# The second factor of a blocked Fourier transform: four separate 32x32 products instead of stacked cosine and sine rows

## The chip, the cores and the metric

The kernel runs on one core of a Trainium2 chip. A core has a matrix engine (PE; its weight loads are listed as PEld), a vector engine (DVE), an activation engine (ACT), a general engine (POOL) and a queue engine (SP); each works through its own instructions in order, and they meet through semaphores. PE writes to PSUM only, and PSUM has eight banks, each holding 512 floats in every one of 128 partitions. The metric is the time of one execution on the device in microseconds (us).

## The reference

The input x has 8 batches of 3008 rows and 256 channels. Each batch is filtered along its rows in the frequency domain, and the result goes through two dense layers with an ELU between them, all in float32.

```python
X = np.fft.rfft(x, axis=1)
Y = X * (filt_r + 1j * filt_i)[None, :, :]
y = np.fft.irfft(Y, n=x.shape[1], axis=1)
h = y.reshape(8 * 3008, 256) @ w_in                       # to 2048
g = np.where(h > 0.0, h, np.exp(np.minimum(h, 0.0)) - 1.0)
return g @ w_out                                          # to 256
```

## The kernel before

**The transform.** 3008 is 64 times 47, so the transform is two factors with a trip through DRAM between them. For one batch: `x_unit` and `a_unit` do the first factor forward (length 64, six pieces c, two to an `a_unit`), and `z_write` puts the result z into DRAM. `z_read` brings back four rows of it for one step g of 0 to 7, `f_read` the filter for that step, `b_unit` does the second factor forward (length 47, folded to 24 cosine and 24 sine rows) and multiplies by the filter. `bi_unit` does the second factor back for two steps together, `y_write` and `y_read` go through DRAM again, and `n_unit` does the first factor back for a sixth of the batch (m of 0 to 5). `n_sums` prepares it for the dense layers.

**The dense layers.** They are done by Strassen-Winograd 2x2 blocks with seven products: `up_steps` gives seven steps s1, s2, s6, s5, s7, s3, s4 of the first layer for a quarter q of the 2048 columns, `down_steps` seven steps of the second layer. A step is two matmul instructions in the code and four in the trace. One pass of seven ups and seven downs is called a quad here: quad i does the ups of item i (b, m, q) and the downs of item i - 1. The steps share PSUM banks: s1, s6, s5 and s3 add up in one bank (phs), s7 and s4 in one (phd), s2 has one (pha). ACT copies phs out after s1, s6 and s5; DVE adds what was copied to pha and phd (L502); ACT takes exponentials in two instructions (L511, L512); DVE takes the maximum (L516); after the steps comes a tail of four DVE sums (L552 to L556). s4 adds into phd only when the DVE add of s7 has read it. DVE adds the second layer's result up in three instructions in the quad after q = 3 and four more in `c_unit`, both at L592, and `o_unit` transposes it (L614, two instructions) and sends it out in 16 DMAs (L624).

**The order.** The order of all instructions is written out by hand. A batch has a period of 24 quads; `at(quad, place, ...)` puts a piece of transform work into a quad, at place 0 (after seven or eight of its 14 steps) or place 1 (at its end). The transform of batch b runs in the 24 quads of batch b - 1's dense layers; below, quads are counted 0 to 23 within that period. The steps go

```python
for k in "DUUDUDDU" if i in opens else "UUDUDDU":    # place 0 follows
for k in "DUUDUD" if i in opens else "DUUDUDD":      # place 1 follows
```

with U an up and D a down. A quad in `opens` begins with a down, which needs none of the four PSUM banks (`banks`, tiles m0 to m3) that ups, `a_unit`, `n_unit`, `b_unit` and `bi_unit` take in turn from the front of one list and return to its end; the other four banks hold the second layer's sums. In a period `a_unit` stands at the end of quads 2, 4 and 7, `b_unit` at the end of quads 9, 10, 12, 13, 15, 16, 18 and 19, `bi_unit` at the end of 11, 14, 17 and 20, and `n_unit` in quads 23, 1, 5, 8, 12 and 16.

**The step that changes.** In `b_unit` a step's input lies in 48 rows twice: cosine rows above sine rows, for the real part (`LO`) and the imaginary part (`HI`). Sixteen matmuls (L376) of 48 rows, 32 columns of weights and 256 moving columns leave both parts in two PSUM banks (psr, psi). DVE multiplies both by both filter parts (`products`, L328 to L331), and POOL does the sums (L385 to L390), with three copies more in step 0 (L393, L395). `z_read` issues four DMAs a step on SP, `f_read` four on POOL.

Of the kernel before, what the change touches and what calls it, by code (L numbers as in the profile page):

```python
# [41 lines left out]
def _make_tables():  # L42
# [53 lines left out]

    fb, bb = np.zeros((P, 2, 2, 32)), np.zeros((P, 2, 4, 32))
    for r in (LO, HI):  # L100
        fb[r, :, 0, :24] = gb[r, :, 0:24]
        fb[r, 0, 1, 1:24] = gb[r, 0, 24:47]
        fb[r, 1, 1, :24] = gb[r, 1, 24:48]
    for o in range(0, P, 32):
        for p, (t, c) in enumerate(((gr, 0), (gr, 24), (gi, 0), (gi, 24))):
            bb[o:o + 24, 0, p, :24] = t[0:24, 0, c:c + 24]

    bb[0:24, 1, 0, :24], bb[0:24, 1, 1, :24] = gr[0:24, 1, 0:24], gr[24:48, 1, 24:48]
    bb[0:24, 1, 2, :24], bb[0:24, 1, 3, :24] = gi[24:48, 1, 0:24], gi[0:24, 1, 24:48]
    pairs = np.concatenate([fb.reshape(P, P), bb.reshape(P, 2 * P)], 1)  # L110
    lie = np.concatenate([2 * np.arange(24), 2 * np.arange(24) + 1])
    gb[:, :, lie] = gb[:, :, :48].copy()
    for t in (gr, gi):
# [15 lines left out]
def kernel(  # L129
# [22 lines left out]
    sdp = pool("sdp", 2)  # L152
    tnp = pool("tnp", 2)
    t1p = pool("t1p", 3)
    t2p = pool("t2p", 2)
    sp = pool("sp", 1)
    qp = pool("qp", 1)
    t3p = pool("t3p", 1)
# [5 lines left out]
    psO = pool("psO", 1, space=PSUM)  # L164
    psM = pool("psM", 1, space=PSUM)

    pairs = glob.tile([P, 3 * P], FP32, name="pairs")
    fb = pairs[:, 0:P].rearrange("p (v c k) -> p v c k", v=2, c=2)
    bb = pairs[:, P:3 * P].rearrange("p (v a i) -> p v a i", v=2, a=4)

    w_in, w_out = ([glob.tile([P, 7, 2, P], FP32, name="%s%d" % (n, i)) for i in range(4)] for n in ("wi", "wo"))

    fbufs = [glob.tile([P, 2, 2, D], FP32, name="f%d" % i) for i in range(FBUFS)]
    edges = glob.tile([P, 2], FP32, name="edges")
    fd = fdp.tile([NG, 2, 48, 2, 2, D], FP32, name="fd")
    fp = fdp.tile([NG, 4, 24, 2, 2, D], FP32, name="fp")

    xs, tas, tns, t1s, t2s, ss, t3s, t4s, zs, yds, ys, g_of, po_of, cs_, sds = ({} for _ in range(15))

    def raw(src, row, ap, col=0):  # L180
        return bass.AP(tensor=src.tensor, offset=src.offset + row * D + col, ap=ap)
# [98 lines left out]

    def t_first(g):

        pool, tag = (t4p, "t4") if g % 4 > 1 else (t2p, "t2")
        t = t2s[0, g] = pool.tile([P, 4, D], FP32, tag=tag, name="t2")
        for j in range(2):
            i = j + 2 * (g % 2 if g < 4 else 0)
            ps = psO.tile([P, 2, 256], FP32, tag="po%d" % i, name="po%d" % i)
            for u in range(2):
                k = 4 * g + 2 * j + u
                for dh in range(2):  # L290
                    nc.tensor.transpose(ps[0:ROWS, u, ts(dh, P)], zt[k // 16][dh][:, ts(k % 16, ROWS)], eye)
            nc.scalar.activation(out=t[0:ROWS, 2 * j:2 * j + 2, :], in_=ps[0:ROWS], func=AXT.Copy)
# [10 lines left out]
            nc.sync.dma_start(z[r], t[HALVES[r]])  # L303

    def z_read(b, g):
        t = t2s[b, g] = t2p.tile([P, 4, D], FP32, tag="t2", name="t2")
        for p, r in enumerate((0, 24, 64, 88)):
            k = p * K2 + 4 * g
            nc.sync.dma_start(t[r:r + 24].rearrange("i u d -> i (u d)"), zs[b][:, k:k + 4, :].rearrange("i u d -> i (u d)"))

    def f_read_first(g, t):
        for a, r in enumerate((LO, HI)):
            nc.gpsimd.dma_start(t[r].rearrange("p c u d -> p (c u d)"), fd[g, a].rearrange("q c u d -> q (c u d)"))

    def f_read(b, g):
        t = fbufs[(b * NG + g) % FBUFS]
        for a in range(4):
            nc.gpsimd.dma_start(t[32 * a:32 * a + 24].rearrange("p c u d -> p (c u d)"),
                                fp[g, a].rearrange("q c u d -> q (c u d)"))
# [47 lines left out]


    def b_unit(b, g):
        t = t2s.pop((b, g))  # L370
        f = fbufs[(b * NG + g) % FBUFS]
        (i0, re), (i1, im) = (bank(n) for n in ("psr", "psi"))
        for c in range(2):
            for a in range(4):
                for ps, k in ((re, LO), (im, HI)):
                    nc.tensor.matmul(ps[32 * a:32 * a + 32, c, :], fb[k, 1 if g == a == 0 else 0, c, :], t[k, a, :],  # L376
                                     start=True, stop=True)
        sr, si = (sp.tile([P, 2, D], FP32, tag=n, name=n) for n in ("sr", "si"))
        if g % 2 == 0:
            ss[b, g] = qp.tile([P, 4, 2, D], FP32, tag="z", name="zs")  # L380
        z = ss[b, g - g % 2][:, :, g % 2]
        p, q = z[:, 0:2], z[:, 2:4]
        products(re, im, f, sr, si, p, q)
        banks.extend((i0, i1))
        nc.gpsimd.tensor_tensor(out=sr, in0=sr, in1=p, op=ALU.add)  # L385
        nc.gpsimd.tensor_tensor(out=p[:, 0], in0=sr[:, 0], in1=sr[:, 1], op=ALU.add)
        nc.gpsimd.tensor_tensor(out=p[:, 1], in0=sr[:, 0], in1=sr[:, 1], op=ALU.subtract)
        nc.gpsimd.tensor_tensor(out=si, in0=si, in1=q, op=ALU.add)
        nc.gpsimd.tensor_tensor(out=q[:, 0], in0=si[:, 0], in1=si[:, 1], op=ALU.subtract)
        nc.gpsimd.tensor_tensor(out=q[:, 1], in0=si[:, 0], in1=si[:, 1], op=ALU.add)  # L390
        if g == 0:

            nc.gpsimd.tensor_copy(out=p[0:32], in_=sr[0:32])  # L393
            for i in range(2):
                nc.gpsimd.tensor_copy(out=q[0:32, i], in_=si[0:32, 1 - i])  # L395

# [233 lines left out]
    def w_fetch(k, queue=nc.gpsimd):  # L632
        q, j = divmod(k, 4)

        if k in (3, 4):
            wd = t2p.tile([P, 4, D], FP32, tag="t2", name="wd").rearrange("p u d -> p (u d)")
        elif k in (10, 11):
            wd = t1p.tile([P, XC, D], FP32, tag="t1", name="wd").rearrange("p u d -> p (u d)")
        elif k in (6, 7, 8, 9):
            wd = xp.tile([P, 2, 2, D], FP32, tag="xc", name="wd").rearrange("p k u d -> p (k u d)")  # L640
        else:
            wd = fbufs[{5: 0, 12: 1, 13: 2, 14: 0, 15: 1}.get(k, k)].rearrange("p c u d -> p (c u d)")
        wd = wds[k] = wd.bitcast(U32).rearrange("p (a w) -> p a w", w=2)
        if j < 2:
            srcs = [moe_w_in.bitcast(U32)[ts(j, P), ts(q, 1024)]]
        else:
            srcs = [moe_w_out.bitcast(U32)[ts(4 * q + 2 * (j - 2) + i, P), :] for i in range(2)]
        for i, s in enumerate(srcs):
            n = 512 // len(srcs)
            queue.dma_start(wd[:, ts(i, n), :].rearrange("p a w -> p (a w)"), s)  # L650
# [79 lines left out]
    def f_pairs(c, u):  # L730

        src = fd.rearrange("g a q c u d -> (g a) q c u d")[:, :, c, u, :]
        dst = fp.rearrange("g (a u) k c h d -> (g a) u k c h d", u=2)[:, u, :, c, :, :]
        nc.gpsimd.dma_start(dst[:, :, 0, :], src[:, 0:48:2, :])
        nc.gpsimd.dma_start(dst[:, 1:24, 1, :], src[:, 1:46:2, :])
        nc.gpsimd.dma_start(dst[:, 0, 1, :], src[:, 47, :])
        if u == 0:
            nc.gpsimd.dma_start(dst[0, :, 1, :], src[0, 1:48:2, :])

    with tc.manual_schedule():  # L740


        with tc.tile_pool(name="boot", bufs=1) as bp:
# [3 lines left out]
            gs = bp.tile([P, 3, 2, 64], FP32, name="gs")  # L747
            gr, gi = gs[:, 1], gs[:, 2]
            zq = qp.tile([P, 4, 2, D], FP32, tag="z", name="zq")
            pqs = [[(sp if i == 0 else bp).tile([P, 2, D], FP32, name="s%s" % n, **({"tag": "s" + n} if i == 0 else {}))  # L750
                    for n in "ri"] +
                   [zq[:, 0:2, i], zq[:, 2:4, i]] for i in range(2)]
            t3f = t3p.tile([P, 2, 4, D], FP32, tag="t3", name="t3")
            zt[0] += [bp.tile([P, 16 * ROWS], FP32, name="zt%d" % i) for i in range(2)]

# [104 lines left out]
        def at(quad, place, fn, *a):  # L860
            plan.setdefault((quad, place), []).append((fn, a))
# [8 lines left out]
        for c in range(2):  # L870
            for u in range(2):
                at(1 + 2 * c + u, 0, f_pairs, c, u)
        for i, f in enumerate(fbufs):
            at(3 + i, 1, nc.vector.memset, f, 0.0)
        for b in range(B):
            t = (b - 1) * PER
            if b > 0:
                for c, s in enumerate((2, 2, 4, 4, 7, 7)):
                    at(t + s, 0, x_unit, b, c)
                    if c % 2 == 0:  # L880
                        opens.add(t + s + 1)
# [2 lines left out]
                    if nb < B:  # L884
                        at(t + s, 1, x_load, nb, nxt)
                    at(t + s, 1, z_write, b, c)
                for g in range(NG):
                    s = t + 9 + g + g // 2
                    at(s, 1, b_unit, b, g)
                    at(s - 2, 1, f_read, b, g)  # L890
                    at(s - 2, 1, z_read, b, g)
                    if g % 2:

                        opens.add(s + 2)
                        at(s + 1, 1, bi_unit, b, g - 1)
                        at(s + 1, 1, y_write, b, g - 1)
            for m, (s, place) in enumerate(((23, 0), (25, 1), (29, 1), (32, 0), (36, 0), (40, 0))):
                if b > 0 or m > 0:
                    at(t + s - 2, 0, tn_read, b, m)
                    at(t + s - 2, 0, y_read, b, m)  # L900
                    at(t + s, place, n_unit, b, m)

                    at(*((t + s + 1, 1) if m == 5 else (t + s, place)), n_sums, b, m)
                at(t + PER + 4 * m + 5, 0, c_unit, b, m)
                at(t + PER + 4 * m + 6, 0, o_unit, b, m)

        items = [(b, m, q) for b in range(B) for m in range(6) for q in range(4)]
        for i in range(-PER, len(items) + 3):
            ups, up_tail = up_steps(*items[i]) if 0 <= i < len(items) else ((), None)
            downs, down_tail = down_steps(*items[i - 1]) if 1 <= i <= len(items) else ((), None)  # L910
            ups, downs = list(ups), list(downs)
            for k in "DUUDUDDU" if i in opens else "UUDUDDU":
                s = ups if k == "U" else downs
                if s:
                    s.pop(0)()
            for fn, a in plan.get((i, 0), ()):
                fn(*a)
            for k in "DUUDUD" if i in opens else "DUUDUDD":
# [41 lines left out]
```

## Time and profile before

| what | value |
| --- | --- |
| median of 3 runs | 2620.88 us (2619.74 to 2622.86) |
| the profiled execution, from its first to its last instruction | 2618.7 us; what the runs' median has beyond that is 2.2 us |
| granted PE clock, mean | 0.994 |
| PE busy | 2569.9 us, 98% |
| PEld busy | 2220.2 us, 85% |
| DVE busy | 1852.8 us, 71% |
| ACT busy | 1504.0 us, 57% |
| POOL busy | 486.9 us, 19% |

The page gives no time of the profiled execution other than its span, so the span stands for it. A group of instructions is named by line, engine, operation and output<-inputs. "128x512" is partitions by elements; for a matmul "24*32 24x512" is rows by columns of weights and rows by columns of the moving operand. A duration is that of one instruction from start to end; instructions on one engine overlap a little, so where a queue is added up the text uses the distance from start to start. "Idle before" is the time that an engine stood before an instruction, and the name behind it is what ended it.

### The profile page before, as it was taken

How to read it: one execution, taken by the hardware profiler on the slowest of the kernel's cores; microseconds unless marked ns; L12 is line 12 of the kernel's file. 1: busy time of each engine (PE TensorE's matmuls, PEld its weight loads, DVE VectorE, ACT ScalarE, POOL GpSimd, SP SyncE). 2: the span in 40 equal slices, each digit the busy share in tenths (PEclk: the TensorE clock that was granted, in tenths of full speed). 3: DMA queues.
4: the chain of work that ended last, by engine and by line, in shares of the span. 5: the costliest groups of instructions: out<-in, count | busy, mean ns of one | idle time of the engine just before them, and what ended most of it. 6: DMA issues, size and time to landing. Idle time of an engine off the chain costs nothing.

```text
span 2618.7 us, 41226 instructions
## 1 busy us (share of the span) xinstructions
PE 2569.9 (98%) x15300; PEld 2220.2 (85%) x15300; DVE 1852.8 (71%) x3203; ACT 1504.0 (57%) x2622; POOL 486.9 (19%) x669
## 2 busy tenths in 40 slices
PE   6799999999999999999999999999999999999998
PEld 4688889888898888988889888998889888898887
DVE  6876776677666776777667767677677667766666
ACT  7665555655555555555555555555555555555554
POOL 5102330024100331004300134002330023300000
PEclk9899999999999999999999999999999999999999
DMA  9544222432224232333314331143321332210010
GB/s 296 169 115 105 63 63 55 117 83 70 66 62 115 63 92 48 82 90 80 79 45 104 83 98 45 45 111 96 86 61 40 87 85 63 63 41 20 22 28 17
DMA packets 228840, 206.51 MB, mean 79 GB/s; under 512 B 130962, under 2 KB 194674, under 8 KB 228640
## 3 DMA queue, kind: packets, MB, share of 16 engines
q1 hardware_dynamic: 211328, 166.90, 25.4%
q0 software_dynamic: 15856, 36.25, 4.9%
q8 instruction: 121, 1.98, 0.3%
q10 hardware_dynamic: 1456, 0.72, 0.1%
q14 instruction: 79, 0.65, 0.1%
HBM read 131.91 MB, written 78.17 MB: 80 GB/s over the span
## 4 chain that ended last, share of the span: by engine, by line
PE 96%; DMA 0%; DVE 0%; ACT 0%; issue 0%; DVEq 0%; SPq 0%; ACTq 0%
PE po L576 44%; PE phs L494 25%; PE phd L494 12%; PE pha L494 6%; PE psn L443 3%; PE psr L376 2%; PE psa L228 2%; PE pv L409 1%; PE po L324 0%; DMA yd<-t 0%; PE psi L376 0%; DMA t<-yd 0%; PE psr L324 0%; DVE c L592 0%; PE psi L324 0%
## 5 line engine op out<-in xcount | busy, mean ns | idle before, releaser
L576 PE MATMUL po<-g,wo 128*128 128x256 f32 (+1 forms) x5376 | 1306.1, 376 | 0.0
L576 PEld LDWEIGHTS po<-g,wo 128*128 128x128 f32 x5376 | 1016.2, 190 | 139.1 <-issue 20.0
L505 ACT ACTIVATE g<-phs 128x512 f32<-128x512 f32 (+1 forms) x576 | 339.3, 589 | 819.2 <-PE phs L494 819.1
L502 DVE TENSOR_TENSOR g<-phd,g 128x512 f32<-128x512 f32 (+1 forms) x384 | 259.4, 675 | 413.3 <-ACT e L512 322.2
L512 ACT ACTIVATE e<-e 128x512 f32<-128x512 f32 (+1 forms) x768 | 477.2, 621 | 24.3
L516 DVE SCALAR_TENSOR_TENSOR g<-e,g 128x512 f32<-128x512 f32 (+1 forms) x576 | 400.5, 695 | 1.3 <-ACT e L512 1.3
L494 PE MATMUL phs<-y,wi 128*128 128x256 f32 (+1 forms) x1536 | 394.5, 380 | 0.0
L494 PE MATMUL phs<-ys,wi 128*128 128x256 f32 (+1 forms) x1536 | 387.9, 375 | 1.5 <-ACT g L505 1.5
L511 ACT ACTIVATE e<-g 128x512 f32<-128x512 f32 (+1 forms) x576 | 353.2, 613 | 35.7 <-DVE g L502 26.6
L494 PEld LDWEIGHTS phs<-y,wi 128*128 128x128 f32 x1536 | 284.9, 191 | 55.1 <-issue 11.5
L494 PEld LDWEIGHTS phs<-ys,wi 128*128 128x128 f32 x1536 | 291.9, 190 | 34.9 <-ACT g L505 2.5
L385 POOL TENSOR_TENSOR sr<-sr,zs 128x512 f32<-128x512 f32 x56 | 71.3, 1273 | 1131.7 <-DVE zs L330 1131.7
L516 DVE SCALAR_TENSOR_TENSOR g<-e,phs 128x512 f32<-128x512 f32 (+1 forms) x192 | 129.9, 677 | 128.5 <-ACT e L512 128.5
L511 ACT ACTIVATE e<-phs 128x512 f32<-128x512 f32 (+1 forms) x192 | 112.9, 588 | 147.7 <-PE phs L494 147.7
L494 PE MATMUL phd<-ys,wi 128*128 128x256 f32 (+1 forms) x768 | 194.6, 376 | 0.0
L494 PE MATMUL phd<-y,wi 128*128 128x256 f32 (+1 forms) x768 | 193.8, 375 | 0.0
L494 PE MATMUL pha<-y,wi 128*128 128x256 f32 (+1 forms) x768 | 193.8, 375 | 0.0
L494 PEld LDWEIGHTS phd<-ys,wi 128*128 128x128 f32 x768 | 145.4, 190 | 19.0 <-DVE g L502 3.0
L494 PEld LDWEIGHTS pha<-y,wi 128*128 128x128 f32 x768 | 146.1, 190 | 16.3
L494 PEld LDWEIGHTS phd<-y,wi 128*128 128x128 f32 x768 | 146.1, 190 | 16.2
L502 DVE TENSOR_TENSOR g<-pha,g 128x512 f32<-128x512 f32 (+1 forms) x192 | 129.2, 673 | 40.5 <-PE pha L494 40.2
L553 DVE TENSOR_TENSOR g<-g,g 128x512 f32<-128x512 f32 (+1 forms) x192 | 130.7, 681 | 6.7
(129 smaller groups left out, 2356.5 us busy)
## 6 DMA issues: line engine op xcount, KB each, us to landing
yd<-t SPq DMA_DIRECT2D x127, 192.0 KB
t<-yd SPq DMA_DIRECT2D x190, 128.0 KB
z<-t SPq DMA_DIRECT2D x84, 256.0 KB
f<-fp POOLq DMA_DIRECT2D x224, 96.0 KB, 3.1
t<-z SPq DMA_DIRECT2D x224, 96.0 KB
out_dram<-o SPq DMA_DIRECT2D x632, 32.0 KB
tn<-tn_t SPq DMA_DIRECT2D x48, 256.0 KB
xc<-in_x_dram SPq DMA_DIRECT2D x84, 128.0 KB
```

Source lines behind the costliest of these rows:

```text
L228: nc.tensor.matmul(p[o:o + 64, u, :], w[r, u, o:o + 64], src[r, u, :], start=True, stop=True)
L376: nc.tensor.matmul(ps[32 * a:32 * a + 32, c, :], fb[k, 1 if g == a == 0 else 0, c, :], t[k, a, :], start=True, stop=True)
L385: nc.gpsimd.tensor_tensor(out=sr, in0=sr, in1=p, op=ALU.add)
L443: nc.tensor.matmul(ps[:, ts(q, P)], t[:, i - 4 * m, ds(dh * P, P)], w[:, i - 4 * m, :], start=True, stop=True)
L494: nc.tensor.matmul(ps[:, a, 0:h], w_in[q][:, COMBO[n], a, :], y[n], start=start and a == 0, stop=True, skip_group_check=True)
L502: nc.vector.tensor_tensor(out=g[o], in0=i0, in1=i1, op=ALU.add)
L505: nc.scalar.activation(out=g[o], in_=i0, func=AXT.Copy)
L511: nc.scalar.activation(out=e, in_=src, func=AXT.Relu, scale=-1.0)
L512: nc.scalar.activation(out=e, in_=e, func=AXT.Exp, scale=-1.0)
L516: nc.vector.scalar_tensor_tensor(out=g[n], in0=es[n], scalar=1.0, in1=src, op0=ALU.subtract, op1=ALU.max)
L553: nc.vector.tensor_tensor(out=b12, in0=b22, in1=b12, op=ALU.subtract)
L576: nc.tensor.matmul(po[i][:, u, 0:h], w_out[q][:, COMBO[n], a, :], g[n][:, a, :], start=q == 0 and a == 0 and n in (1, 3, 6, 4), stop=True, ...
```

## The change

`b_unit` takes two steps g and g + 1 at once. The four products (cosine and sine of the real and of the imaginary part) are computed apart, each from 24 rows in its own group of 32 partitions, in 16 matmuls of 24 rows, 32 weight columns and 512 moving columns (40 traced instructions rather than 32 where g is 0). They fill all four banks. ACT copies two of them out, and DVE adds and subtracts the other two. The filter products are split into `re_mult` and `im_mult`, the sums into `re_sums` and `im_sums`, all on DVE; POOL keeps only DMAs and memsets. Step 0 has eight ACT copies more, for its first 32 partitions (four of them in `b_unit`, straight after the two large ones). A new place 2 follows the third step of a quad. Per period: `b_unit` at the end of quads 6, 10, 14 and 18, `re_mult` and `re_sums` in the next quad at places 2 and 1, `im_mult` and `im_sums` likewise in the one after, `bi_unit` at the end of quads 9, 13, 17 and 21, and the quads after `b_unit` and after `bi_unit` are in `opens`. `x_unit` and `a_unit` move to quads 0, 2 and 4 (2, 3 and 4 for b = 1). `z_read` and `f_read` are issued for two steps together, one and two quads ahead of `b_unit`. `y_read` of m = 0 moves from quad 21 to quad 22; `n_sums` of m = 3 and 4 moves to the end of the next quad. The input and filter buffers become fixed tiles, and one DMA of `f_pairs` reads zeros.

```diff
     def b_unit(b, g):
-        t = t2s.pop((b, g))
-        f = fbufs[(b * NG + g) % FBUFS]
-        (i0, re), (i1, im) = (bank(n) for n in ("psr", "psi"))
+        pf = [bank("pf") for _ in range(4)]
+        both = [(a, p, slice(1 if g == a == 0 else 0, 2), 0) for a in range(4) for p in range(4)]
+        if g == 0:
+            both = [(0, p, slice(0, 1), 1) for p in range(4)] + both
+        for a, p, js, v in both:
+            r = slice(32 * p, 32 * p + 24)
+            nc.tensor.matmul(pf[p][1][32 * a:32 * a + 32, js, :], fb[r, v, :], t2[r, js, a, :],
+                             start=True, stop=True, tile_position=(32 * p, 32 * a))
+        t = rs[b, g] = sp.tile([P, 4, 2, D], FP32, tag="r", name="r")
+        c, s, ci, si = (ps for _, ps in pf)
+        for k, ps in ((1, c), (3, si)):
+            nc.scalar.activation(out=t[:, k], in_=ps, func=AXT.Copy)
+        if g == 0:
+            for k, ps in ((0, c), (2, si), (1, s), (3, ci)):
+                nc.scalar.activation(out=once_in[0:32, k], in_=ps[0:32, 0, :], func=AXT.Copy)
+        for k, ps in ((0, s), (2, ci)):
+            nc.vector.tensor_tensor(out=t[:, k], in0=t[:, k + 1], in1=ps, op=ALU.add)
+            nc.vector.tensor_tensor(out=t[:, k + 1], in0=t[:, k + 1], in1=ps, op=ALU.subtract)
+        banks.extend(pf[p][0] for p in (0, 3, 1, 2))
+
+    def re_mult(b, g):
+        t, f = rs[b, g], fall[:, 0:2]
+        z = ss[b, g] = qp.tile([P, 4, 2, D], FP32, tag="z", name="zs")
+        if g == 0:
+            nc.scalar.activation(out=t[0:32, :, 0, :], in_=once_in[0:32], func=AXT.Copy)
         for c in range(2):
-            for a in range(4):
-                for ps, k in ((re, LO), (im, HI)):
-                    nc.tensor.matmul(ps[32 * a:32 * a + 32, c, :], fb[k, 1 if g == a == 0 else 0, c, :], t[k, a, :],
-                                     start=True, stop=True)
...
-        products(re, im, f, sr, si, p, q)
-        banks.extend((i0, i1))
-        nc.gpsimd.tensor_tensor(out=sr, in0=sr, in1=p, op=ALU.add)
-        nc.gpsimd.tensor_tensor(out=p[:, 0], in0=sr[:, 0], in1=sr[:, 1], op=ALU.add)
-        nc.gpsimd.tensor_tensor(out=p[:, 1], in0=sr[:, 0], in1=sr[:, 1], op=ALU.subtract)
-        nc.gpsimd.tensor_tensor(out=si, in0=si, in1=q, op=ALU.add)
-        nc.gpsimd.tensor_tensor(out=q[:, 0], in0=si[:, 0], in1=si[:, 1], op=ALU.subtract)
-        nc.gpsimd.tensor_tensor(out=q[:, 1], in0=si[:, 0], in1=si[:, 1], op=ALU.add)
...
+            nc.vector.tensor_tensor(out=z[:, 2 + c], in0=t[:, c], in1=f[:, :, 0, c, :], op=ALU.mult)
+            nc.vector.scalar_tensor_tensor(out=z[:, c], in0=t[:, 2 + c], scalar=-1.0, in1=f[:, :, 1, c, :],
+                                           op0=ALU.mult, op1=ALU.mult)
+
+    def re_sums(b, g):
+        z = ss[b, g]
+        for c in range(2):
+            nc.vector.tensor_tensor(out=z[:, 2 + c], in0=z[:, 2 + c], in1=z[:, c], op=ALU.add)
+        for c, op in ((0, ALU.add), (1, ALU.subtract)):
+            nc.vector.tensor_tensor(out=z[:, c], in0=z[:, 2], in1=z[:, 3], op=op)
...
+    def im_mult(b, g):
+        t, f = rs[b, g], fall[:, 0:2]
+        for c in range(2):
+            nc.vector.tensor_tensor(out=t[:, c], in0=t[:, c], in1=f[:, :, 1, c, :], op=ALU.mult)
+            nc.vector.tensor_tensor(out=t[:, 2 + c], in0=t[:, 2 + c], in1=f[:, :, 0, c, :], op=ALU.mult)
+
+    def im_sums(b, g):
+        t, z = rs.pop((b, g)), ss[b, g]
+        for c in range(2):
+            nc.vector.tensor_tensor(out=t[:, c], in0=t[:, c], in1=t[:, 2 + c], op=ALU.add)
+        for c, op in ((0, ALU.subtract), (1, ALU.add)):
+            nc.vector.tensor_tensor(out=z[:, 2 + c], in0=t[:, 0], in1=t[:, 1], op=op)
...
-                for c, s in enumerate((2, 2, 4, 4, 7, 7)):
+                for c, s in enumerate((2, 2, 3, 3, 4, 4) if b == 1 else (0, 0, 2, 2, 4, 4)):
...
-                for g in range(NG):
-                    s = t + 9 + g + g // 2
+                for g in range(0, NG, 2):
+                    s = t + 6 + 2 * g
+                    opens.update((s + 1, s + 4))
+                    for k in (g, g + 1):
+                        at(s - 2, 0, f_read, b, k)
+                        at(s - 1, 0, z_read, b, k)
                     at(s, 1, b_unit, b, g)
...
+                    at(s + 1, 2, re_mult, b, g)
+                    at(s + 1, 1, re_sums, b, g)
+                    at(s + 2, 2, im_mult, b, g)
+                    at(s + 2, 1, im_sums, b, g)
+                    at(s + 3, 1, bi_unit, b, g)
+                    at(s + 3, 1, y_write, b, g)
...
-                    at(t + s - 2, 0, y_read, b, m)
+                    at(t + s - (1 if m == 0 else 2), 0, y_read, b, m)
...
-                    at(*((t + s + 1, 1) if m == 5 else (t + s, place)), n_sums, b, m)
+                    at(*((t + s + 1, 1) if m > 2 else (t + s, place)), n_sums, b, m)
```

## The prediction

> **What bounds the kernel now.** I read the page's busy times and its chain first, then the chain in order of time, the waits, and the timelines of PE, DVE, ACT and SP around single units.
>
> ```profile
> PE 2569.9 (98%) x15300; PEld 2220.2 (85%) x15300; DVE 1852.8 (71%) x3203; ACT 1504.0 (57%) x2622; POOL 486.9 (19%) x669
> ...
> PE 96%; DMA 0%; DVE 0%; ACT 0%; issue 0%; DVEq 0%; SPq 0%; ACTq 0%
> ```
>
> PE carries the chain. That it is busy does not prove that it never waits, so I build a period from its pieces. In the chain in order of time the same `a_unit` returns after one period:
>
> ```profile
> 763.72 1.89 PE psa L228 x32
> ...
> 1080.12 1.89 PE psa L228 x32
> ```
>
> That is 316.40 us. Four traced matmuls of a step start 0.865 apart from the next step's (0.757 at 224 columns), so 20 quads of 14 steps at 12.10 and four at 10.60 make 284.5. Six `n_unit` at 1.785, three `a_unit` at 2.05, eight `b_unit` at 1.20 and four `bi_unit` at 1.26 (0.2 more for g = 0) bring it to 316.3. So hardly 0.2 us a period is waiting: PE time saved counts in full, and so does every new wait of PE. The two prices that matter, from PE's timeline:
>
> ```profile
> 856.87 1.13 PE L494 MATMUL phs<-y,wi 128*128 128x256 f32 x4
> ...
> 870.17 1.13 PE L494 MATMUL phs<-y,wi 128*128 128x256 f32 x4
> ```
> ```profile
> 922.81 1.89 PE L576 MATMUL po<-g,wo 128*128 128x256 f32 x8
> 924.63 1.14 PE L409 MATMUL pv<-zs,pairs 24*32 24x512 f32 x32
> 925.70 1.13 PE L576 MATMUL po<-g,wo 128*128 128x256 f32 x4
> ```
>
> A quad that ends in `b_unit` takes 13.30, so `b_unit` costs 1.20. `bi_unit` takes from 922.81 + 2 x 0.865 = 924.54 to 925.70, and the step behind it 0.10 more than usual: 1.26.
>
> The second thing to see is where DVE stands when a quad ends (here PE's steps end at 937.92):
>
> ```profile
> 937.42 0.68 DVE L502 TENSOR_TENSOR g<-phd,g 128x512 f32<-128x512 f32 x1
> ...
> 941.27 0.69 DVE L556 TENSOR_TENSOR g<-g,g 128x512 f32<-128x512 f32 x1
> 941.88 0.68 DVE L328 TENSOR_TENSOR sr<-psr,f 128x512 f32<-128x512 f32 x1
> ```
>
> After a quad in `opens` DVE is free 3.97 after PE's last step, after another quad 3.1 (858.85 against 855.75). And there is one place where DVE already holds up PE, s4 waiting for the add of s7:
>
> ```profile
> PEld phd L494 <- DVE g L502: 3.0, 8, 0.4
> ```
>
> **The change, part by part.** *PE.* The new `b_unit` has `bi_unit`'s shape exactly (24 rows, 32 columns, 512 moving, row groups changing fastest), so I take 1.26 for two steps, and 1.46 for g = 0 with its 40 instructions. Bounds: `a_unit`, the nearest unit that packs less well, 2.05; the old unit 1.20. Before: 8 x 1.20 + 4 x 1.26 + 0.2 = 14.84; after: 8 x 1.26 + 0.4 = 10.48. Saved 4.36 a period, 30.5 us in seven (22 us less at 2.05, 2 us more at 1.20; I take the row of the same shape).
>
> *DVE.* Per pair of steps eight products leave and 20 instructions come: four sums from PSUM, eight products, eight sums. Independent ones start 0.60 apart, dependent ones 0.72. So 2.4 (`b_unit`), 2.4 + 2.54 (`re`), 2.4 + 2.54 (`im`), 12.3 against 4.8 before. Four quads have 4 x 6.9 of ELU work, 5.6 for second layer, transposes and `n_sums`, and now 12.3: 45.5 of some 52.7 us of PE. DVE stays under PE on average, at 86%; the question is the order. I walk one group, counted from each quad's first PE step.
>
> Quad s + 1 (opens): tail free at 2.6 (3.97 less the unit), PSUM sums to 5.0, add of s2 to 5.6, `re_mult` to 8.0. s7 ends only at 8.74, so nothing is late; the gap in which DVE used to wait for ACT and PE (1.4 to 5.4 us before that add) swallows it. For g = 0, `re_mult` also waits for an ACT copy of 32x1024, between 0.60 (128x512) and 3.62 (128x4096), about 0.9 by length: from 5.0 to 5.9, so `re_mult` ends at 8.3, still in time; behind it in ACT's queue is the copy after s6 (ends 5.2, 0.8 later at g = 0), which s5 needs at 7.0 plus that 0.8. At 3.62 both would be late by about 2 us a period. The other small copies have a quad to spare. Quad s + 2: tail free at 3.97, `re_sums` to 6.5, add of s2 to 7.1, `im_mult` to 9.5, add of s7 ready at 10.25 (0.68 and 0.06 for the semaphore). s4 starts at 9.51 in a plain quad, at 11.3 in one with `n_unit`. Quads 8, 12 and 16 have `n_unit`; quad 20 has none and waits 0.74. Quad s + 3: the three second-layer adds and `im_sums` come before its add of s2, which ends at 7.35; `c_unit`'s four take 1.47, and the add of s7 is ready at 9.5 against s4 at 9.51. No wait, but no room either. I put 0.1 a period. The exponentials follow the s2 add: at 7.2 in quad s + 2, they and four ACT copies end at 10.5, when s3 ends. `bi_unit` at the end of s + 3 needs the sums that ended at 6.8.
>
> *Banks.* The new unit needs all four. In opens quads (10, 14, 18) one down follows s4 instead of two, and the fourth bank is read until 938.10 where the unit could start at 938.0: 0.12 each, 0.36 a period; behind it on PE stand the unit's rest and the whole next quad. Behind it ACT copies two tiles at 0.55 each; s1 comes after one down, 0.97 later, and its bank is out by then. For g = 0 two large copies and one small one (bounds: 0.38 for 128x256, nothing) stand before that bank is returned: 0.24 + 1.1 + 0.4 = 1.75 against 0.97, a wait of 0.8 a period.
>
> *POOL.* Six sums a step go (1272 ns and 730 ns each in the trace); nothing of PE waited for them. While they ran, a DVE instruction on two SBUF operands took 1.16 instead of 0.68 (L516 at 908.41), and PE lost 0.16 behind it; with the rest, 0.2 a period comes back. The page "SBUF — State Buffer" of the Trainium skill (SBUF: two separate sides) states that DVE and GpSimd share a port pair as an exclusive lock; by it all of L516's 710 - 688 ns over 480 instructions, 10.6 us of DVE, would return, beside PE. `f_read`'s eight DMAs now wait for `im_mult` and land three quads before use; the same DMAs left DVE at 0.68 at 247 to 251, so I cost them nothing. If they were late, `re_mult` and all of DVE behind it would stand.
>
> *SP.* `z_read` issues eight DMAs (3.2 us) 1.5 quads, 19 us, before use: nothing. `y_read` of m = 0 moves behind `o_unit`'s 16 DMAs in quad 22. From `bi_unit`'s end: copies out to 2.3, `y_write` issued to 5.3, outs to 12.8 (7.45 for 16), `y_read` to 14.7, its last landing 3 to 3.5 after its issue as in the first batch (91.97 plus 3.72), so 17.3 to 17.8. `n_unit` starts at 12.2 + 6.05 = 18.3. Nothing, with 0.5 us of cover; where the 16 take 8.8, as at 918.52, it costs 0.5 to 1. Behind the waiting `y_read` stand the reads of m = 1, used a quad and more later.
>
> *x_unit, a_unit, n_sums, zeros, buffers.* Same instructions, other quads. Loads get 1.5 quads (18 us) at least, in b = 1; they are issued in 10 us and `a_unit` stays on PE at 2.05. DVE's 2.6 us for two pieces now falls in quads without the new work. Nothing, with 2 us either way for the boot's altered buffers.
>
> *Sum.* A period: -4.36 + 0.74 + 0.1 + 0.36 + 0.8 - 0.2 = -2.56; seven are -17.9. On the profiled execution 2618.7 - 17.9 = 2600.8 of span, and with the 2.2 us by which the runs' median exceeds the span, 2603.
>
> *A rule against it.* The wait at g = 0 is PE waiting for evacuation, in 7 of 28 new units. "TensorEngine Tiling (Array Packing)" of the Trainium skill (Performance Considerations, PSUM Bottleneck) says that tiling speeds up the matmuls and not the evacuation, which may become the bottleneck. By it the 0.8 would stand behind all 28 units, 17 us more: 2620. The existing `bi_unit`, with four copies and a total of 3.2 us in 21 waits, speaks for the lower figure.
>
> **The rivals.** *DVE backlog (slower).* The add of s7 in quads s + 3 has no slack and quad 20 none. Everything by which DVE is later than in my walk is paid by PE five times a period, 35 times in all: 35 us per us. 0.5 us more gives 2620, 0.66 the bound of slower, 1 us 2638. For it: the margin of 0.01. Against: all durations are measured ones, and DVE falls back into step at the exponential of s3, whose wait it cannot pass.
>
> *y_read late.* 1.5 us a period, 10.5 in all: 2613. For: 16 DMAs ahead in SP's queue. Against: the walk above.
>
> *Full cover.* Quad 20, the banks and g = 0 cost half of what I put (the bank waits overlap the unit's own start): 1.0 us less a period, 2596; none of them at all, 2590.
>
> *The change doesn't save PE time*, the new unit at 2.05 and its waits as above: 22 us less saved, 2625.
>
> **How the numbers follow.** A measurement tells about 0.2%, 5.2 us, from no change. Forecast 2598 to 2611: 0.46. Full cover: 0.17. y_read: 0.10, faster for two thirds of it. Unit not shortened: 0.05, same. DVE backlog: 0.22, of which 0.06 faster or same and 0.16 slower. Faster 0.46 + 0.17 + 0.07 + 0.01 = 0.71, cut to 0.68 for what I have not seen in the order; same 0.14; slower 0.18. The range leaves out 0.07 below (no waits and a shorter unit) and 0.13 above (a backlog of over 0.7 us): 2590 to 2628.
>
> **What would show it.** PE's new group at L409's shape with 952 traced matmuls, each unit 1.07 long; the period at 313.8. In the waits, PE for DVE's L502 in quad 20 and PE for ACT after g = 0. DVE busy up by 28 x 12 instructions of 0.68, to about 2080; POOL down by its sums' 339 to about 150. Wrong would be: PE idle before s4 in quads 9, 13, 17 and 21, or `n_unit` waiting for a DMA, or a unit that takes 2 us.

## The result

The change makes the kernel slower: 2715.07 us, median of 4 runs (2712.67 to 2717.67), against 2620.31 us for the kernel before in the same session; the ratio is 1.036, with a 95% interval of 1.0345 to 1.0375. The forecast was 2603. The profiled execution has a span of 2714.1 us, 95.4 more than before. The page's busy times and chain:

```profile
PE 2584.7 (95%) x14460; PEld 2221.4 (82%) x14460; DVE 2043.7 (75%) x3538; ACT 1558.1 (57%) x2734; POOL 156.0 (6%) x312
...
PE 82%; DVE 7%; SPq 3%; ACT 3%; issue 1%; DMA 1%; DVEq 0%; ACTq 0%
```

PE's share of the chain is down from 96% to 82%: PE now waits. The waits name for what (engine and line, what it waited for, us in total, times, the longest):

```profile
PE phs L528 <- ACT g L539: 71.2, 16, 5.0
PE psa L276 <- DMA tn<-tf_t: 15.0, 2, 13.1
PE psn L477 <- DMA t<-yd: 14.6, 7, 10.1
PE phd L528 <- DVE g L536: 4.7, 8, 0.6
```

```profile
ACT zs L429 <- DVE zs L426: 39.7, 14, 5.5
ACT zs L413 <- DVE zs L411: 35.7, 7, 5.1
```

The first line is the result: a matmul into phs waits 5 us for ACT's copy of phs (L539), twice in each of the seven periods. The second block says why ACT was late: L413 and L429 are the three small copies of step 0 behind `re_sums` and `im_sums`, and they wait for DVE. The second line of the first block and the 10.1 us of the third lie in the first 97 us, where the kernel before had its waits for loads and weights too.

Here is the first of the two gaps on PE, ACT and DVE (start, duration, instruction, and in brackets the idle time before it). Quad 8 begins at 861.39:

```profile
862.25 1.03 PE L528 MATMUL pha<-y,wi 128*128 128x256 f32 x4
863.12 1.03 PE L610 MATMUL po<-g,wo 128*128 128x256 f32 x4
869.16 2.07 PE L528 MATMUL phs<-ys,wi 128*128 128x256 f32 x4 [5.02 <-ACT g L539]
871.03 3.62 PE L610 MATMUL po<-g,wo 128*128 128x256 f32 x8
```

```profile
862.28 0.63 ACT L546 ACTIVATE e<-e 128x512 f32<-128x512 f32 x1
868.01 0.63 ACT L413 ACTIVATE zs<-zs 32x512 f32<-32x512 f32 x1 [5.10 <-DVE zs L411]
868.54 0.57 ACT L539 ACTIVATE g<-phs 128x512 f32<-128x512 f32 x1
```

```profile
865.36 1.28 DVE L409 TENSOR_TENSOR zs<-zs 128x512 f32<-128x512 f32 x2
866.68 1.29 DVE L411 TENSOR_TENSOR zs<-zs 128x512 f32<-128x512 f32 x2
```

DVE finishes `re_sums` at 867.97, 6.6 us into the quad, close to the 6.5 of the forecast. ACT's next instruction in order is the copy L413, which needs these sums. It starts at 868.01, and only behind it comes the copy of phs after s1, whose operand had been ready since 862.4, when s1 ended. s6 adds into phs, so it may not start before; it starts at 869.16 instead of 863.98. The same happens in quad 9 behind `im_sums`.

Then the clock. s6 and the two downs behind it take twice as long as usual: two downs take 3.41 from 871.03 instead of 1.73. The busy times by stretch (length; busy us of PE, PEld, DVE, ACT and POOL; the granted clock is the column before the last two) show it:

```profile
866.00:870.00 4.00, 0.84 (x2) 0.75 (x3) 2.79 (x6) 1.11 (x2) 0.00 (x0) 0.77 0.00 0
870.00:876.00 6.00, 6.00 (x19) 4.85 (x19) 2.24 (x4) 0.81 (x2) 3.47 (x8) 0.58 0.23 71
876.00:884.00 8.00, 8.00 (x45) 7.22 (x44) 3.81 (x7) 7.05 (x13) 0.45 (x1) 1.00 0.16 48
```

A period can be read off `n_unit` of m = 0 in the chain in order of time:

```profile
750.39 2.02 PE psn L477 x16
...
1080.64 2.02 PE psn L477 x16
```

It is 330.25 us, where 313.84 was forecast and 316.40 measured before. Counted from where s6 would have started, the first gap of this period is 5.17 (5.02 of it shown as idle) and the slow steps behind it add 2.96; the second has 5.10 and 2.24: 15.5 us together. `n_unit` of m = 0 starts 0.66 late and runs 0.24 longer: 0.9. Together 16.4, which is the whole difference from the forecast.

### The profile page after: what moved, and what is told of

The parts are those of the page before. It is cut to its first block, busy times and chain, and to the rows that moved or that the text cites. A ratio compares the mean times of both kernels' runs of the same rounds, so it can differ in the third digit from the quotient of the medians.

```text
span 2714.1 us, 39654 instructions
## 1 busy us (share of the span) xinstructions
PE 2584.7 (95%) x14460; PEld 2221.4 (82%) x14460; DVE 2043.7 (75%) x3538; ACT 1558.1 (57%) x2734; POOL 156.0 (6%) x312
## 4 chain that ended last, share of the span: by engine, by line
PE 82%; DVE 7%; SPq 3%; ACT 3%; issue 1%; DMA 1%; DVEq 0%; ACTq 0%
PE po L610 37%; PE phs L528 22%; PE phd L528 11%; PE pha L528 5%; PE psn L477 3%; SPq L658 2%; PE psa L233 1%; DVE g L550 1%; PE pf L382 1%; PE pv L443 1%; DVE g L536 1%; DMA t<-yd 1%; SPq L454 1%; DVE zs L409 1%; ACT e L546 1%
## 5 line engine op out<-in xcount | busy, mean ns | idle before, releaser
L610 PE MATMUL po<-g,wo 128*128 128x256 f32 (+1 forms) x5376 | 1330.3, 380 | 0.0
L539 ACT ACTIVATE g<-phs 128x512 f32<-128x512 f32 (+1 forms) x576 | 338.6, 588 | 786.8 <-PE phs L528 786.8
L528 PE MATMUL phs<-ys,wi 128*128 128x256 f32 (+1 forms) x1536 | 403.5, 386 | 71.2 <-ACT g L539 71.2
L528 PEld LDWEIGHTS phs<-ys,wi 128*128 128x128 f32 x1536 | 298.8, 196 | 112.7 <-ACT g L539 77.8
L528 PE MATMUL phs<-y,wi 128*128 128x256 f32 (+1 forms) x1536 | 388.8, 376 | 0.5
L550 DVE SCALAR_TENSOR_TENSOR g<-e,g 128x512 f32<-128x512 f32 (+1 forms) x576 | 387.3, 672 | 0.8 <-ACT e L546 0.2
L550 DVE SCALAR_TENSOR_TENSOR g<-e,phs 128x512 f32<-128x512 f32 (+1 forms) x192 | 129.8, 676 | 127.9 <-ACT e L546 126.9
L323 POOL DMA_DIRECT2D fall<-fp x224 | 110.0, 499 | 1401.6 <-DVE r L419 1327.0
```

Source lines behind the costliest of these rows:

```text
L528: nc.tensor.matmul(ps[:, a, 0:h], w_in[q][:, COMBO[n], a, :], y[n], start=start and a == 0, stop=True, skip_group_check=True)
L539: nc.scalar.activation(out=g[o], in_=i0, func=AXT.Copy)
L550: nc.vector.scalar_tensor_tensor(out=g[n], in0=es[n], scalar=1.0, in1=src, op0=ALU.subtract, op1=ALU.max)
L610: nc.tensor.matmul(po[i][:, u, 0:h], w_out[q][:, COMBO[n], a, :], g[n][:, a, :], start=q == 0 and a == 0 and n in (1, 3, 6, 4), stop=True, ...
```

## The experiments

Two theories were put against each other. *ACT's order*: three small copies stand in ACT's queue before their operands are ready, and the copy of phs behind them holds up PE. *DVE backlog*, the forecast's rival: DVE with POOL's sums on top is simply too late.

**The copies later.** In the changed kernel all three copies are put at place 0 of the quad after; `re_once` holds the copy of `re_sums`, `im_once` the two of `im_sums`:

```diff
+                    if g == 0:
+                        at(s + 2, 0, re_once, b, g)
                     at(s + 2, 2, im_mult, b, g)
...
+                    if g == 0:
+                        at(s + 3, 0, im_once, b, g)
                     at(s + 3, 1, bi_unit, b, g)
```

> Edit: of the changed kernel, the three small ACT copies of step 0 behind the sums (one in re_sums, two in im_sums) are put into ACT's queue at place 0 of the following quad instead of at the end of their own. Nothing else moves. Theory (ACT works in order; these copies wait for DVE sums that end 6 to 7 us into the next quad, the copy of phs after s1 is queued behind them, s6 cannot start, and PE's clock drops behind each gap): both gaps of about 5.1 us and the slow steps behind them, 3.0 and 2.2 us, go in each of seven periods, 15.5 x 7 = 108 us, so about 2607, granted clock back near 0.99. Rival (DVE as a whole is too late after taking over POOL's sums, so PE waits somewhere in any case): the wait moves to another line and the time stays above 2680.

2616.84 us, a ratio of 0.9982 (0.9973 to 0.9992) to the kernel before. 98 us come back, a little more than the 95 lost, by moving 21 copies of at most 0.63 us each. Not one instruction of DVE was taken away, so a backlog of DVE is not what cost the time. The largest waits of PE that reach into the periods now (10.1 us of the first line belong to the start):

```profile
PE psn L481 <- DMA t<-yd: 14.9, 7, 10.1
PE phd L532 <- DVE g L540: 4.7, 8, 0.6
```

The result stays 10 us above the 2607 expected. The slow steps give back a little less than 15.5 a period on average (329.9 against 315.1, so 14.8), and in the two profiled executions the first `n_unit` started at 95.44 and 99.11: the start waits for DMAs and differs between executions by up to 4.8 us (95.03 to 99.80 in all profiles of this study).

**One copy of the three.** Only the copy of `re_sums` is moved.

```diff
+                    if g == 0:
+                        at(s + 2, 0, re_once, b, g)
                     at(s + 2, 2, im_mult, b, g)
```

> Edit: only the copy of re_sums is put later, those of im_sums stay. In-order theory: the first of the two gaps goes, 5.17 + 2.96 = 8.1 us a period, 57 us, so about 2658; the second gap, in the quad after, stays as it is. Rival (DVE backlog): the second gap, which comes after more DVE work, grows or the time hardly moves, above 2690.

2666.75 us, 48 less than the changed kernel and 50 more than with all three moved. The profile has seven gaps of 5.12 left, all in quad 9. The gaps add up; a gap costs about 7 us with its slow steps, not quite the 8.1 expected.

**The wait put into the kernel before.** POOL's three copies of step 0 are done by ACT, in the same place:

```diff
-            nc.gpsimd.tensor_copy(out=p[0:32], in_=sr[0:32])
+            nc.scalar.activation(out=p[0:32], in_=sr[0:32], func=AXT.Copy)
             for i in range(2):
-                nc.gpsimd.tensor_copy(out=q[0:32, i], in_=si[0:32, 1 - i])
+                nc.scalar.activation(out=q[0:32, i], in_=si[0:32, 1 - i], func=AXT.Copy)
```

> Edit: the kernel before, with the three copies of step 0 that POOL does moved to ACT, in the same place of the program. DVE, PE and the PSUM banks are as before. In-order theory: ACT's copy of phs after s1 now waits behind them for POOL's sums, which end 10.0 us into the quad in the trace of before; copies and phs copy end at 11.6, s6 could have started at 2.7: a gap of 9 us a period and some 3 us of slow clock behind it, 84 us, so about 2704; without a clock effect 63 us, 2683. Rival (DVE's new work is the cause): no change, 2620.

2693.83 us, 71.9 more than the kernel before (ratio 1.0271, 1.0256 to 1.0287), with none of the change in it. ACT's timeline shows the same picture, with POOL's sums in the place of DVE's:

```profile
886.33 0.63 ACT L393 ACTIVATE zs<-sr 32x512 f32<-32x512 f32 x1 [7.25 <-POOL zs L387]
888.35 0.41 ACT L395 ACTIVATE zs<-si 32x256 f32<-32x256 f32 x1 [1.39 <-POOL zs L389]
889.03 0.41 ACT L395 ACTIVATE zs<-si 32x256 f32<-32x256 f32 x1 [0.27 <-POOL zs L390]
889.35 0.57 ACT L505 ACTIVATE g<-phs 128x512 f32<-128x512 f32 x1
```

The copy of phs starts 9.8 us into the quad. PE waits 7.7 rather than 9: POOL's sums end 0.6 earlier than in the trace of before (its last sum takes 0.72 instead of 1.26, with DVE waiting), and only the last of the three copies still stands behind them. 71.9 / 7 = 10.3 a period leaves 2.5 for the slow steps.

**A shorter gap.** The copies stand one step further back, behind ACT's copy after s1 and ahead of that after s6 (place 2 of the same quads).

```diff
-                        at(s + 2, 0, re_once, b, g)
+                        at(s + 2, 2, re_once, b, g)
...
-                        at(s + 3, 0, im_once, b, g)
+                        at(s + 3, 2, im_once, b, g)
```

> Edit: like late_copies, but the copies stand at place 2, behind the phs copy of s1 and ahead of that of s6. In-order theory: now s5 waits, until 7.9 and 8.6 us into the two quads instead of 5.2: gaps of 2.6 and 3.4 us, 6.0 x 7 = 42 us above late_copies, about 2649, if gaps of this length do not lower the clock; up to 36 us more if they lower it as the gaps of 5 us did. Rival (DVE backlog): the place of three small ACT copies matters little, the same as late_copies within 10 us.

2654.84 us, 38 more than with the copies at place 0, so the place matters as ACT's order says. There are 14 gaps of 2.35 to 2.43; the second of a period was expected at 3.4 and is 2.35. In the 8 us behind them the granted clock is 1.00 eleven times and 0.79 three times; two of them, in one period:

```profile
848.50:856.50 8.00, 8.00 (x45) 7.29 (x46) 4.27 (x8) 6.06 (x11) 3.93 (x8) 1.00 0.40 100
864.99:872.99 8.00, 8.00 (x29) 6.84 (x30) 3.65 (x8) 4.12 (x7) 0.00 (x0) 0.79 0.00 0
```

**The copies on DVE.** In the changed kernel DVE does the three copies itself, where ACT did them.

```diff
-            nc.scalar.activation(out=z[0:32, 0:2, 0, :], in_=z[0:32, 2:4, 0, :], func=AXT.Copy)
+            nc.vector.tensor_copy(out=z[0:32, 0:2, 0, :], in_=z[0:32, 2:4, 0, :])
...
-                nc.scalar.activation(out=z[0:32, 2 + c, 0, :], in_=t[0:32, 1 - c, 0, :], func=AXT.Copy)
+                nc.vector.tensor_copy(out=z[0:32, 2 + c, 0, :], in_=t[0:32, 1 - c, 0, :])
```

> Edit: the changed kernel with the three copies of step 0 behind the sums on DVE instead of ACT, in the same place of the program; DVE gets 1.0 to 1.6 us more a period. In-order theory: DVE wrote the operands itself, so nothing on ACT waits: 2617 as in late_copies, and up to 0.8 us a period more in quad 9, where the add of s7 has no slack, 2617 to 2623. Rival (DVE backlog): DVE gets even more work, so slower than the changed kernel, above 2715.

2617.33 us, a ratio of 0.9983 (0.9974 to 0.9992). DVE gets more work, and still the time falls by 98 us against the changed kernel. The rival is out. The price that the expectation allowed for is there but small: s4 now waits for DVE's add of s7 15 times rather than 8, 7.0 us in the run rather than 4.7.

**The rest of the shortfall.** With the copies at place 0, `y_read` of m = 0 is put ahead of the 16 output DMAs again:

```diff
-                    at(t + s - (1 if m == 0 else 2), 0, y_read, b, m)
+                    at(t + s - 2, 1 if m == 0 else 0, y_read, b, m)
```

> Edit: late_copies, and y_read of m = 0 is issued at the end of quad 21, straight behind y_write and ahead of the 16 output DMAs of quad 22. Theory (what is left of the shortfall is y_read behind those 16 DMAs: in late_copies n_unit of m = 0 starts 0.64 us late and takes 0.24 us longer for its reads in each period): 0.9 x 7 = 6 us less than late_copies, about 2610 to 2611. Rival (the reads are late because y_write is, not because of the queue): as late_copies, 2617.

2609.39 us, ratio 0.995 (0.9937 to 0.9962), 7.5 less. The waits of `n_unit` for its reads behind the start are gone; the one of 9.9 us at the start remains.

**The two waits that the forecast had named.** On top of that, the first two additions of `re_sums` go to place 0 of their quad as `re_adds`, and in step 0 the small copy out of a bank follows the large one of the same bank.

```diff
-                    at(s + 1, 1, re_sums, b, g)
+                    at(s + 1, 0, re_adds, b, g)
+                    at(s + 1, 1, re_sums, b, g)
...
-        for k, ps in ((1, c), (3, si)):
-            nc.scalar.activation(out=t[:, k], in_=ps, func=AXT.Copy)
-        if g == 0:
-            for k, ps in ((0, c), (2, si), (1, s), (3, ci)):
-                nc.scalar.activation(out=once_in[0:32, k], in_=ps[0:32, 0, :], func=AXT.Copy)
+        for k, o, ps in ((1, 0, c), (3, 2, si), (None, 1, s), (None, 3, ci)):
+            if k is not None:
+                nc.scalar.activation(out=t[:, k], in_=ps, func=AXT.Copy)
+            if g == 0:
+                nc.scalar.activation(out=once_in[0:32, o], in_=ps[0:32, 0, :], func=AXT.Copy)
```

> Edit: early_y, and the first two additions of re_sums stand at place 0 of their quad instead of at its end (they then fill DVE's wait before the add of s7 and no longer delay the add of s7 in quad 20), and in step 0 each small ACT copy out of a bank stands straight behind the large one of the same bank. Theory (the three known waits): quad 20 gives back 0.75 us a period, step 0 about 0.5, 8 to 9 us less than early_y, about 2602. Rival (the additions push the add of s7 in the quad after b_unit past s4): a new wait of up to 0.7 us in four quads a period, no gain, 2611 or more.

2599.13 us, ratio 0.9911 (0.9898 to 0.9925): faster than both kernels. Behind the first 100 us a single wait of PE for DVE is left, 0.6 us at 144.46; the granted clock is 0.991, and PE is busy again:

```profile
PE 2548.4 (98%) x14460; PEld 2201.3 (85%) x14460; DVE 2035.1 (78%) x3538; ACT 1552.5 (60%) x2734; POOL 156.2 (6%) x312
```

A period takes 313.02, of which PE is busy 312.93. Of the 10.3 us gained over the version before it, where 8 to 9 were expected, the start gave 2.0 (the first `n_unit` at 97.33 instead of 99.35) and the shorter period 1.22 in each of seven.

**What PE time is worth.** In this version every matmul of the new `b_unit` is issued twice:

```diff
-        for a, p, js, v in both:
+        for a, p, js, v in both + both:
```

> Edit: best, with all matmuls of the new b_unit issued twice (the second pass writes the same values again). Theory (PE is the bound, so a unit's PE time counts in full; the forecast's saving of 30 us was real and was hidden by the waits): 28 units with 0.86 to 1.07 us more each, 24 to 30 us, so 2623 to 2629. Rival (the b phase is now bound by DVE, at 85% and more of its quads): much of it is hidden, less than 10 us more, under 2609.

2634.2 us, 35 more. The profile prices the doubled unit: 2.39 from its start to the next step, 1.21 without doubling (the first two lines are from the version without, the last two from that with it).

```profile
867.21 1.28 PE L382 MATMUL pf<-t,pairs 24*32 24x512 f32 x32
868.42 1.13 PE L617 MATMUL po<-g,wo 128*128 128x256 f32 x4
...
876.53 2.45 PE L382 MATMUL pf<-t,pairs 24*32 24x512 f32 x64
878.92 1.13 PE L617 MATMUL po<-g,wo 128*128 128x256 f32 x4
```

That is 1.17 a unit (1.13 for step 0), 32.5 us for 28 units; the period grows by 4.9, 34 us in seven. The expectation was low by its price of a unit (0.86 to 1.07), but not in kind: PE time still counts in full while DVE has its new work.

## Why the prediction was wrong

The step that failed is one sentence in the walk of DVE's work: "The other small copies have a quad to spare." Their results had: nothing needs them before `bi_unit`. The sentence priced a late result and forgot the queue. ACT works in order, so an instruction that waits holds all behind it (L413 started at 868.01 and L539, ready at 862.4, only behind it), and behind these three stands the copy of phs that s6 needs 2.6 us into the quad. All that was needed for the right price was in the text: `re_sums` end at 6.5 and `im_sums` at 6.8 by its own walk, and the same paragraph asked what stood behind another ACT copy, the one of 32x1024, in just this way, and found it in time. With 6.5 + 0.6 + 0.6 against 2.6 it would have come to two gaps of 5 us a period, 70 us. The rival on the slower side had the wrong engine: PE did not wait for DVE's add of s7, but for ACT behind DVE; of the sign named for it, PE idle before s4 in quads 9, 13, 17 and 21, the changed kernel shows none.

The second part was not foreseen: gaps of 5 us are followed by matmuls at half speed, 1.5 to 3 us for each. The trace of before has no such gap in its periods, but its start could have warned: behind a gap of 3.3 us there (PE back at 70.15) and one of 10.1 (95.93) the granted clock of the next 8 us is 0.60 and 0.72.

```profile
70.15:78.15 8.00, 8.00 (x42) 4.60 (x46) 5.55 (x10) 4.24 (x8) 0.00 (x0) 0.60 0.19 49
95.93:103.93 8.00, 7.36 (x32) 6.72 (x33) 6.53 (x15) 3.44 (x6) 0.68 (x2) 0.72 1.05 292
```

The other terms of the sum, in a period of the changed kernel:

| term | forecast | measured |
| --- | --- | --- |
| three units of g > 0, with the wait for the fourth bank | 4.14 | 4.20 |
| step 0, with its wait | 2.26 | 2.19 |
| quad 20, s4 waiting for the add of s7 | 0.74 | 0.75 |
| `y_read` of m = 0 | 0 | 0.9 |
| ACT copies of step 0 behind the sums | 0 | 15.5 |

The unit on PE, from the previous step's end at 916.36 to 917.66 and 0.10 behind it:

```profile
915.49 1.03 PE L610 MATMUL po<-g,wo 128*128 128x256 f32 x4
916.45 1.28 PE L382 MATMUL pf<-t,pairs 24*32 24x512 f32 x32
917.66 1.13 PE L610 MATMUL po<-g,wo 128*128 128x256 f32 x4
```

Quad 20, where the walk's lag of DVE was right to 0.01 us:

```profile
1044.18 1.03 PE L610 MATMUL po<-g,wo 128*128 128x256 f32 x4
1045.79 1.13 PE L528 MATMUL phd<-ys,wi 128*128 128x256 f32 x4 [0.58 <-DVE g L536]
```

In step 0 the sum was right and its parts were not: the unit took 1.66 instead of 1.36, and s1 waited 0.23 instead of 0.8, so the reordered copies had only 0.2 to give back. For the same reason the rule on evacuation that the prediction weighed would have been the worse price: the waits behind the other 21 units did not appear.

`y_read` failed by the size of one term. The 16 output DMAs of quad 22, issued straight behind `y_write`, took 9.04 to 10.05 us of SP's time, not 7.45. The prediction had set 0.5 to 1 us against 16 that take 8.8, and left it out of the sum:

```profile
1064.05 3.00 SPq L454 DMA_DIRECT2D yd<-t  x4
1067.15 9.06 SPq L658 DMA_DIRECT2D out_dram<-o  x16
1076.26 1.82 SPq L464 DMA_DIRECT2D t<-yd  x4
```

Why they take longer there is not shown. In all 28 places of the changed kernel where the 16 follow straight behind `y_write` they took 9.04 or more, and in the run with `y_read` between the two, 7.53 to 8.18 in quad 22; but the kernel before has up to 8.99 with no `y_write` ahead. That the order costs about 1 us a period (7.5 us in seven) is shown by the run with `y_read` ahead.

So the forecast's saving of PE time was there. The kernel of the diff with its three copies moved is 5 us faster than before. The version that has just the waits of the forecast's sum is the one with `y_read` moved too: 2609.39, 6 above the forecast, with a period of 314.24 against 313.84 (what makes up these 0.4 us was not followed up) and a start that was 3.4 us later than in the profile of before. The 2599.13 of the last version lie 4 below the forecast, but it has shed waits that the forecast counted, so that it comes so near 2603 is no confirmation of the sum.

## What to carry to other kernels

For every instruction that a change adds to an engine working in order, price two things: when its result is needed, and what stands behind it in the queue while it waits for its operands. The second is the one that a glance at busy times never shows; ACT was 57% busy in both kernels. When work moves to another engine, look for the small follow-ups that stay behind and now wait across engines; let the engine that wrote the operand do them, or put them where the operand is certain to be there.

## What the runs showed of the hardware

A gap of 4.9 to 5.1 us on PE was followed by a lower granted clock in all 21 cases of two kernels (0.61 to 0.81 over the next 8 us), the gaps of 7.5 to 7.6 in all seven (0.63 to 0.82), and gaps of 2.35 to 2.43 in three of 14. While the clock is down, steps take twice their time. "TensorE: Matmul & The Clock Gate" of the Trainium skill (HAM oscillation — how this bites in real kernels) advises against idle gaps of over about 3.4 us; these runs agree for the longer gaps, and show the loss now and then for gaps of 2.4 as well. No run was made on what tells the three from the eleven, but the trace does. In each of these traces the instants in the periods at which the granted clock falls lie whole multiples of 3.413 us apart; with the shorter gaps they are 865.00, 1172.20 and 1189.27, 90 and 5 such steps from one to the next. Laid on that grid, the three gaps put 1.98 to 2.35 us of idle time into one step and the eleven at most 1.91. Here are one of the eleven and two of the three, each as a step and the one behind it:

```profile
844.52:847.93 3.41, 1.55 (x8) 1.02 (x6) 3.38 (x7) 0.59 (x2) 0.00 (x0) 1.00 0.00 0
847.93:851.35 3.42, 2.85 (x21) 2.75 (x22) 2.38 (x4) 2.17 (x5) 0.75 (x2) 1.00 0.02 5
861.59:865.00 3.41, 1.06 (x6) 0.58 (x5) 3.34 (x7) 1.31 (x3) 0.00 (x0) 1.00 0.00 0
865.00:868.41 3.41, 3.41 (x8) 2.78 (x9) 1.07 (x3) 1.27 (x3) 0.00 (x0) 0.50 0.00 0
1168.79:1172.20 3.41, 1.43 (x9) 1.33 (x10) 3.41 (x7) 1.36 (x3) 0.00 (x0) 1.00 0.00 0
1172.20:1175.61 3.41, 3.41 (x17) 3.23 (x16) 0.39 (x1) 2.62 (x6) 2.74 (x6) 0.50 0.30 89
```

PE is busy 1.55 of 3.41 us in the first step, and the clock stays up; it is busy 1.06 and 1.43 in the others, and the clock is at half in the step that follows. The 28 longer gaps fit as well: the clock falls at the end of the first step with over 2 us idle, and one step with 1.99 idle did not lower it, so the edge in these runs is near 2 us. Whether a gap of 2.4 us lowered the clock thus went by its place on the grid, not by its length. This is read from the traces afterwards; no gap was moved to try it.

With POOL's sums gone, DVE's maximum L550 on two SBUF operands takes 672 ns in the mean where L516 took 695 (576 instructions each, all shapes), 13 us of DVE time a run where the prediction had worked out 10.6. PE was what bounded the last version, so this DVE time lay beside it; no run prices it by itself.
